# Outputs from a decayed state by quarters of the array, and short chunks with two heads stacked, in a fused retention and two-layer kernel

## The chip, the cores and the metric

The kernel runs on one core of a Trainium2 chip. The metric is the device time of one execution in microseconds (us). Before the change it is 884.49 us, the median of 3 runs (883.37 to 885.73).

## What is computed

Retention with a decay per head, its output laid out as 2304 tokens of 512, then two feed-forward layers. Everything is float32.

```python
def _attn_ref(q, k, v):                      # each (4, 8, 576, 64)
    scores = scale * np.matmul(q, k.transpose(0, 1, 3, 2))
    gamma = 1.0 - 2.0 ** (-5.0 - np.arange(H, dtype=np.float32))
    Dmat = np.where(rel >= 0, gamma[:, None, None] ** rel[None, :, :], 0.0)
    return np.matmul(scores * Dmat[None, :, :, :], v)

def _moe_ref(x, w_in, w_out, alpha):         # 512 -> 2048 -> 512
    h = x @ w_in
    g = np.maximum(h, 0.0) + alpha * np.minimum(h, 0.0)
    return g @ w_out

def _moe2_ref(x, w_gate, w_val, w_out):      # 512 -> 1536 -> 512
    gate = 1.0 / (1.0 + np.exp(-(x @ w_gate)))
    return (gate * (x @ w_val)) @ w_out
```

`reference` puts attention's heads beside each other, `x = attn_out.transpose(0, 2, 1, 3).reshape(B * S, H * D)`, and applies the two layers one after the other.

## The kernel before, in words

The 2304 tokens are cut into five blocks (256, then four of 512). Attention works in chunks of at most 128 positions of one sequence within one block, 20 in all; four of them have 64 positions (the end of a sequence of 576, or what a block leaves over). The first block has two chunks, the second five, the later ones four, five and four.

Within a sequence a chunk takes what lies before it from a state of 64x64 per head, kept in `m_sb`. Heads go in four pairs: one head of a pair on partitions 0 to 63, the other on 64 to 127. Before, `m_sb` holds for each pair a 128x128 block with the two heads' states on its diagonal and zeros elsewhere (cleared once, L1132). A chunk runs through these steps:

- `load_qk`, `load_kv` (L461 to L485): q and k with the head's dimensions on the partitions, k and v with the positions on the partitions. A short chunk fills 64 columns of each 128 in `qk`, and 64 partitions of `kv`.
- `att_q`, `att_v` (L488 to L500): POOL multiplies q by the decay and v by its inverse.
- `att_scores` (L502 to L518): TensorE forms k against q for each head, into two banks of PSUM (`s`), and VectorE multiplies both by the causal mask (L514).
- `att_values` (L520 to L563): the outputs from the state (L529, 128x128 operands, one per pair), the sums k against v that update it (L535, tile `m`), VectorE's additions to `m_sb` (L543, or copies for a sequence's first chunk, L545), ScalarE's scaling of `m_sb` by the decay over the chunk (L549), the outputs from the chunk itself (L553), and the split of the output (`split`, L198 to L204) into a high and a low part, one on ScalarE (L200) and one on VectorE (L201).

The layers' matmuls all come from one helper, `products` (L633): three products of high and low parts in the fp32r type. `h` is the first layer's inner value and turns in the two banks of `ps_h`; `y` is its output. A matmul of two float32 operands leaves two records in the trace.

What stands around the chunks differs. `att_run` (L594) takes the seven chunks of the first two blocks one after the other, the scores two chunks ahead, each with banks of its own: the pairs of banks rotate, one pair of `ps_a` and twice two of `ps_y`. Beside them it begins to prepare the first layer's weights: `weight_step` (L439) collects credit, and from the chunk with index `WITH` on (L60, L1160) each step adds 0.34 of a weight. A weight arrives as 512 KB in one of five raw slots (`r`), goes through ScalarE (L223, L224) and VectorE (L227, L229), is split into two parts (L246, L248), and frees its slot. The later three blocks' chunks run in the middle of the first layer (`att_stages`, L580): scores behind one `y`, the rest behind the next `h`.

TensorE's instructions run in the order of the code. The order of the others' queues is set by a scheduler in the compiler, which places an instruction where it expects its inputs; every queue runs strictly in order.

Of the kernel before, what the change touches and what calls it, by code (L numbers as in the profile page):

```python
# [10 lines left out]
F32 = mybir.dt.float32  # L11
# [3 lines left out]
AF = mybir.ActivationFunctionType  # L15
ALU = mybir.AluOpType
# [3 lines left out]
P = 128  # L20
B, H, S, D = 4, 8, 576, 64
NPAIR = H // 2
NT = B * S
DM = 512
KC = DM // P
NF1 = 2048 // P
# [17 lines left out]
PLAIN = 3  # L44
# [12 lines left out]

BEHIND = 2

WITH = 3  # L60


PACE_B, PACE_C = 0.34, 0.5
# [29 lines left out]
O_M = NPAIR * P  # L93
O_GK = O_M + P
O_GP = O_GK + H
N_CST = O_GP + len(LENGTHS) * NPAIR


def constants():
    gamma = (1.0 - 2.0 ** (-5.0 - np.arange(H, dtype=np.float32))).astype(np.float64)  # L100
    i = np.arange(P)
    head = 2 * np.arange(NPAIR)[None, :] + (i // D)[:, None]
    out = np.zeros((P, N_CST), np.float32)
    out[:, :O_M] = (gamma[head][:, :, None] ** i / np.sqrt(D)).reshape(P, -1)
    out[:, O_M:O_GK] = i[None, :] >= i[:, None]
    out[:, O_GK:O_GP] = gamma ** -i[:, None].astype(np.float64)
    out[:, O_GP:] = (gamma[head][:, None, :] ** np.array(LENGTHS)[None, :, None]).reshape(P, -1)
    return out


# [1 line left out]
def retention_two_ffn(ctx: ExitStack, tc: tile.TileContext, att, cst, alpha, w1, w2, out0, out1):  # L112
# [17 lines left out]
    xp = x_only.enter_context(tc.tile_pool(name="xp", bufs=2, side="right"))  # L130
    att_only = ctx.enter_context(ExitStack())
    ap = att_only.enter_context(tc.tile_pool(name="ap", bufs=1))
    c_sb = ap.tile([P, N_CST], F32, tag="c", name="c_sb")
    al_sb = const.tile([P, NF1], F32, tag="al", name="al_sb")
    na_sb = const.tile([P, NF1], F32, tag="na", name="na_sb")
    m_sb = ap.tile([P, NPAIR, P], F32, tag="m", name="m_sb")
# [313 lines left out]
    o = 0  # L450
# [10 lines left out]
    def load_qk(n):  # L461
        if n >= len(CHUNKS):
            return
        c = CHUNKS[n][3]
        half = 2 * c * H * D
        qk = slot([P, 2, NPAIR, P], F32, f"qk{n}")
        a = offset[n]
        src = att[a:a + half].rearrange("(p t a i) -> p t a i", p=P, t=2, a=NPAIR)
        if n == 0:
            nc.sync.dma_start(out=c_sb, in_=cst)  # L470
            nc.sync.dma_start(out=qk[:, :, 0:2, :c], in_=src[:, :, 0:2])
            nc.sync.dma_start(out=qk[:, :, 2:4, :c], in_=src[:, :, 2:4])
        else:
            nc.sync.dma_start(out=qk[:, :, :, :c], in_=src)
        raw_a[n] = [qk, None]

    def load_kv(n):
        if n >= len(CHUNKS):
            return
        c = CHUNKS[n][3]  # L480
        half = 2 * c * H * D
        kv = slot([P, 2, H * D], F32, f"kv{n}")
        a = offset[n] + half
        nc.sync.dma_start(out=kv[:c], in_=att[a:a + half].rearrange("(p t d) -> p t d", p=c, t=2))
        raw_a[n][1] = kv  # L485

    x_t = {}
# [6 lines left out]

    def att_v(n):

        c = CHUNKS[n][3]
        v = raw_a[n][1][:c, 1, :].rearrange("p (h d) -> p h d", h=H)
        gk = c_sb[:c, O_GK:O_GP]
        nc.gpsimd.tensor_tensor(out=v, in0=v, in1=gk.unsqueeze(2).to_broadcast([c, H, D]), op=ALU.mult)  # L500

    def att_scores(n, pool, tags):  # L502

        c = CHUNKS[n][3]
        qk = raw_a[n][0]
        ps = [pool.tile([P, NPAIR, P], F32, tag=tags[e], name=f"s{n}_{e}") for e in range(2)]
        for pr in range(NPAIR):
            for e in range(2):
                r = slice(e * D, (e + 1) * D)
                nc.tensor.matmul(ps[e][:c, pr, :c], qk[r, 1, pr, :c], qk[r, 0, pr, :c], start=True, stop=True)  # L510

        s_sb = qk[:, 1], small.tile([P, NPAIR, P], F32, tag="s", name=f"sc{n}")
        for e in (1, 0):
            nc.vector.tensor_tensor(  # L514
                out=s_sb[e][:c, :, :c], in0=ps[e][:c, :, :c],
                in1=mask[:c, :c].unsqueeze(1).to_broadcast([c, NPAIR, c]), op=ALU.mult,
            )
        return s_sb  # L518

    def att_values(n, s_sb, pool, tags):  # L520

        j, _, pos, c, col = CHUNKS[n]
        qk, kv = raw_a[n]
        last = pos + c == S
        o_ps = pool.tile([P, NPAIR, P], F32, tag=tags[0], name=f"o{n}")

        if pos:
            for pr in range(NPAIR):
                nc.tensor.matmul(o_ps[:, pr, :c], m_sb[:, pr, :], qk[:, 0, pr, :c], start=pr == 0, stop=False)  # L529
        if not last:  # L530
            m_ps = pool.tile([P, NPAIR, D], F32, tag=tags[1], name=f"m{n}")
            for pr in range(NPAIR):
                for e in range(2):
                    h = 2 * pr + e
                    nc.tensor.matmul(  # L535
                        m_ps[e * D:(e + 1) * D, pr, :], kv[:c, 0, h * D:(h + 1) * D],
                        kv[:c, 1, h * D:(h + 1) * D], start=True, stop=True,
                    )
            for e in range(2):
                r = slice(e * D, (e + 1) * D)  # L540
                dst = m_sb[r, :, e * D:(e + 1) * D]
                if pos:
                    nc.vector.tensor_tensor(out=dst, in0=dst, in1=m_ps[r], op=ALU.add)  # L543
                else:
                    nc.vector.tensor_copy(dst, m_ps[r])  # L545

            for pr in range(NPAIR):
                g = O_GP + LENGTHS.index(c) * NPAIR + pr
                nc.scalar.activation(m_sb[:, pr, :], m_sb[:, pr, :], AF.Copy, scale=c_sb[:, g:g + 1])  # L549
        for pr in range(NPAIR):  # L550
            for e in range(2):
                h = 2 * pr + e
                nc.tensor.matmul(  # L553
                    o_ps[e * D:(e + 1) * D, pr, :c], kv[:c, 1, h * D:(h + 1) * D], s_sb[e][:c, pr, :c],
                    start=pos == 0 and pr == 0, stop=pr == NPAIR - 1,
                )
        x = x_t[j]
        if j < PLAIN:
            split(x[:, 0, :, col:col + c], x[:, 1, :, col:col + c], o_ps[:, :, :c], True)
        else:  # L560
            urgent["act"].append(nc.scalar.activation(x[:, :, col:col + c], o_ps[:, :, :c], AF.Copy))
        free(qk)
        free(kv)  # L563

# [564 lines left out]
        split(g[:, 0], g[:, 1], ps[1])  # L1129
        return g  # L1130

    nc.gpsimd.memset(m_sb, 0.0)  # L1132
    for n in runs_of(0) + runs_of(1):
        load_chunk(n)
    nc.sync.dma_start(out=al_sb, in_=alpha)
# [269 lines left out]
```

## Time and profile before

| | |
|---|---|
| median of 3 runs | 884.49 us |
| profiled execution | 882.25 us, span 880.1 us |
| TensorE busy | 854.5 us (97%) |
| VectorE, ScalarE, POOL busy | 523.7, 445.1, 115.6 us |
| DMA | 245.00 MB, mean 278 GB/s |

The span runs from the first to the last instruction of the trace. A group of rows is read from the left: time of start, duration, engine, line, operation, what it writes and reads with shapes, how many. What stands in brackets is the time in which the engine was idle ahead of the row, and the instruction whose end released it.

### The profile page before, as it was taken

What the parts mean: (1) busy time and instruction counts of PE and PEld (TensorE: products, weight loads), DVE (VectorE), ACT (ScalarE), POOL (GpSimd) and SP (SyncE); (2) the same over time, 40 slices, a digit from 0 to 9 for tenths busy, and PEclk for the clock granted to TensorE, in tenths of its full rate; (3) what the DMA queues carried; (4) which work ended last, traced back from release to release, by engine and by line L of the source; (5) the groups of instructions that cost most, each with busy time, mean ns of one, the idle gap of its engine ahead of it and who ended that gap; (6) DMA issues with size and microseconds to landing.
All of it is one profiled execution on the core that took longest, in us unless ns stands there. A gap on an engine that the chain in (4) does not pass through costs nothing.

```text
span 880.1 us, 13000 instructions
## 1 busy us (share of the span) xinstructions
PE 854.5 (97%) x4770; PEld 717.7 (82%) x4770; DVE 523.7 (59%) x761; ACT 445.1 (51%) x785; POOL 115.6 (13%) x119
## 2 busy tenths in 40 slices
PE   5789999999999999999999999999999999999998
PEld 5678888888777888878888888887888888888897
DVE  3777774566676658979736565369833333596121
ACT  2698874455564567888525654345332222353111
POOL 6000002444411001115302131000000000000000
PEclk9899999999999999999999999999999999999999
DMA  9879989799996357777996999635697563359970
GB/s 310 284 280 375 383 287 418 294 346 292 352 335 211 132 196 264 253 289 265 380 386 225 384 419 394 272 108 204 238 396 274 191 192 120 139 210 355 394 265 25
DMA packets 89679, 245.00 MB, mean 278 GB/s; under 512 B 13072, under 2 KB 16144, under 8 KB 89616
## 3 DMA queue, kind: packets, MB, share of 16 engines
q1 hardware_dynamic: 89616, 244.17, 75.9%
q8 instruction: 38, 0.62, 0.3%
q14 instruction: 25, 0.20, 0.1%
HBM read 175.98 MB, written 68.16 MB: 277 GB/s over the span
## 4 chain that ended last, share of the span: by engine, by line
PE 81%; DMA 5%; DVE 5%; ACT 5%; issue 2%; SPq 1%; DVEq 0%; ACTq 0%
PE a L633 15%; PE yy L633 10%; PE h L633 9%; PE y L633 8%; PE oa L633 7%; PE z L633 4%; PE b L633 4%; PE e L633 4%; PE c L633 3%; DMA r<-w 3%; PE o L633 2%; PE oc L633 2%; PE ob L633 2%; PE oe L633 2%; PE a_h L633 2%
## 5 line engine op out<-in xcount | busy, mean ns | idle before, releaser
L633 PE MATMUL h<-x,w 128*128 128x512 f32 (+1 forms) x432 | 84.2, 347 | 4.1 <-DVE g L201 3.4
L633 PEld LDWEIGHTS h<-x,w 128*128 128x128 f32 x432 | 67.4, 189 | 15.0 <-DVE g L201 4.4
L302 POOL TENSOR_TENSOR r<-r,r 128x256 f32<-128x256 f32 x36 | 37.8, 1057 | 235.0 <-DVE r L229 225.4
L313 DVE TENSOR_TENSOR q<-r,q 128x512 fp32r<-128x512 f32 x72 | 52.8, 759 | 19.1 <-ACT q L312 18.9
L649 DVE SCALAR_TENSOR_TENSOR h<-h,na_sb,t 128x512 f32<-128x512 f32 (+1 forms) x48 | 32.0, 667 | 48.8 <-ACT h L648 48.8
L633 PE MATMUL y<-g,w 128*128 128x512 f32 x240 | 58.9, 394 | 0.0
L312 ACT ACTIVATE q<-r 128x512 fp32r<-128x512 f32 x72 | 45.6, 666 | 22.3 <-POOL r L302 11.8
L647 ACT ACTIVATE t<-h 128x512 f32<-128x512 f32 (+1 forms) x48 | 25.2, 524 | 61.3 <-PE h L633 61.2
L223 ACT ACTIVATE r<-r 128x512 f32<-128x512 f32 x68 | 45.4, 668 | 20.2 <-DMA r<-w 20.1
L633 PEld LDWEIGHTS y<-g,w 128*128 128x128 f32 x240 | 44.3, 188 | 10.2 <-issue 1.0
L959 DVE TENSOR_TENSOR c<-a,es 128x512 f32<-128x512 f32 x24 | 16.7, 698 | 55.9 <-PE a L633 55.9
L224 ACT ACTIVATE r<-r 128x512 int32<-128x512 uint32 x68 | 45.5, 669 | 0.0
L493 POOL TENSOR_TENSOR qk<-qk,c_sb 128x512 f32<-128x512 f32 (+1 forms) x21 | 24.7, 1178 | 153.3 <-DVE h L649 120.3
L229 DVE CUSTOM_DVE_ANT_0 r<-r,top 128x1024 uint16<-128x1024 uint16 x52 | 37.0, 721 | 2.7
L633 PEld LDWEIGHTS z<-x,zp 128*128 128x128 f32 x288 | 36.0, 191 | 0.9
L633 PE MATMUL z<-x,zp 128*128 128x256 f32 x288 | 36.3, 283 | 0.0
L201 DVE TENSOR_TENSOR g<-h,g 128x512 fp32r<-128x512 f32 (+1 forms) x48 | 28.8, 599 | 12.5 <-ACT g L200 12.0
L200 ACT ACTIVATE g<-h 128x512 fp32r<-128x512 f32 (+1 forms) x48 | 25.2, 524 | 20.8 <-DVE h L649 19.9
L633 PE MATMUL h<-x,v 128*128 128x512 f32 x144 | 35.4, 395 | 0.0
L633 PE MATMUL y<-g,v 128*128 128x512 f32 x144 | 35.1, 393 | 0.0
L302 POOL TENSOR_TENSOR r<-r 128x256 f32<-128x256 f32 x36 | 32.1, 896 | 11.6 <-DVE r L229 10.4
L227 DVE TENSOR_SCALAR top<-r 128x512 uint32<-128x512 uint32 x52 | 24.0, 470 | 13.4 <-ACT r L223 11.6
(457 smaller groups left out, 2199.4 us busy)
## 6 DMA issues: line engine op xcount, KB each, us to landing
tq<-td SPq DMA_DIRECT2D x84, 512.0 KB, 9.0
r<-w SPq DMA_DIRECT2D x68, 512.0 KB, 6.8
wo<-wod SPq DMA_DIRECT2D x42, 512.0 KB, 3.6
v<-w1d SPq DMA_DIRECT2D x40, 512.0 KB, 6.4
td<-q SPq DMA_DIRECT2D x36, 512.0 KB, 4.8
w1d<-w SPq DMA_DIRECT2D x32, 512.0 KB, 7.6
wod<-q SPq DMA_DIRECT2D x24, 512.0 KB, 9.5
zp<-td SPq DMA_DIRECT2D x48, 256.0 KB, 5.2
```

Source lines behind the costliest of these rows:

```text
L200: a = nc.scalar.activation(hi, src, AF.Copy)
L201: d = nc.vector.tensor_tensor(out=lo, in0=src, in1=hi.bitcast(F32), op=ALU.subtract)
L223: nc.scalar.activation(high.bitcast(F32), high.bitcast(F32), AF.Prelu, scale=2.0 ** -112, alpha=2.0 ** 32)
L224: nc.scalar.activation(low.bitcast(I32), low, AF.Copy, scale=2.0 ** -29)
L229: nc.vector.tensor_tensor(out=out.bitcast(I32), in0=low.bitcast(I32), in1=top.bitcast(I32), op=ALU.add)
L302: sub = lambda o, a, b: nc.gpsimd.tensor_tensor(out=o, in0=a, in1=b, op=ALU.subtract)
L312: nc.scalar.activation(part[0], src, AF.Copy)
L313: nc.vector.tensor_tensor(out=part[1], in0=src, in1=part[0].bitcast(F32), op=ALU.subtract)
L493: nc.gpsimd.tensor_tensor(out=q, in0=q, in1=decay[:, part, :c], op=ALU.mult)
L633: nc.tensor.matmul(ps, l, r, start=first and i == 0, stop=last and i == len(todo) - 1, skip_group_check=joins)
L647: nc.scalar.activation(t, ps, AF.Relu)
L649: nc.vector.scalar_tensor_tensor(ps, ps, na_sb[:, f:f + 1], t, ALU.mult, ALU.add)
```

## The change

- The state is kept without its zeros: `m_sb` is 128x(4x64), and its update is an addition and a scaling of the whole tile, both on VectorE. ScalarE's scaling and the clearing on POOL go.
- The outputs from the state are formed head by head with 64x64 operands instead of pair by pair. The output of an odd pair is changed over: its first head is written to partitions 64 to 127 and the second to 0 to 63. Even and odd pairs go to two banks, so that four heads in a row use the four quarters of the array. The rows of the first layer's input weights are put in the order that matches, on the host.
- The output of a chunk lies in two banks and is split in two halves. The sums `m` move to the banks of `ps_h`, and ahead of the outputs from the state.
- Short chunks have two heads stacked on the partitions in `kv` and in the scores: one bank and one masking instead of two, full partitions for v, and a `qk` tile without gaps. They have constants of their own (a stacked mask, a stacked decay: 68 more columns).
- `WITH` is 4, not 3.

```diff
-WITH = 3
+WITH = 4
@@ load_qk, load_kv
-        qk = slot([P, 2, NPAIR, P], F32, f"qk{n}")
+        qk = slot([P, 2, NPAIR, c], F32, f"qk{n}")
...
-            nc.sync.dma_start(out=qk[:, :, :, :c], in_=src)
+            nc.sync.dma_start(out=qk, in_=src)
...
-        kv = slot([P, 2, H * D], F32, f"kv{n}")
+        kv = slot([P, 2, H * c // P, D], F32, f"kv{n}")
@@ att_scores
+        if c < P:
+            ps = pool.tile([P, NPAIR, c], F32, tag=tags[0], name=f"s{n}")
+            for pr, e in HEADS:
+                nc.tensor.matmul(ps[part(e), pr, :], qk[part(e), 1, pr, :], qk[part(e), 0, pr, :], start=True, stop=True)
+            by = c_sb[:, O_M2:O_GK2].unsqueeze(1).to_broadcast([P, NPAIR, c])
+            nc.vector.tensor_tensor(out=qk[:, 1], in0=ps, in1=by, op=ALU.mult)
+            return qk[part(0), 1], qk[part(1), 1]
@@ att_values
-        o_ps = pool.tile([P, NPAIR, P], F32, tag=tags[0], name=f"o{n}")
+        o_ps = [pool.tile([P, 2, c], F32, tag=t, name=f"o{n}_{i}") for i, t in enumerate(tags)]
+        out = lambda pr, e: o_ps[pr % 2][part(e ^ pr % 2), pr // 2, :]
+        rows = lambda t, pr, e: kv[part(e), t, pr] if c < P else kv[:, t, 2 * pr + e]
+        if not last:
+            m_ps = ps_h.tile([P, NPAIR, D], F32, tag="h", name=f"m{n}")
+            for pr, e in HEADS:
+                nc.tensor.matmul(m_ps[part(e), pr, :], rows(0, pr, e), rows(1, pr, e), start=True, stop=True)
         if pos:
-            for pr in range(NPAIR):
-                nc.tensor.matmul(o_ps[:, pr, :c], m_sb[:, pr, :], qk[:, 0, pr, :c], start=pr == 0, stop=False)
+            for pr, e in HEADS:
+                nc.tensor.matmul(
+                    out(pr, e), m_sb[part(e), pr, :], qk[part(e), 0, pr, :], start=pr < 2, stop=False,
+                )
         if not last:
...
+            if pos:
+                nc.vector.tensor_tensor(out=m_sb, in0=m_sb, in1=m_ps, op=ALU.add)
+            nc.vector.tensor_tensor(out=m_sb, in0=m_sb if pos else m_ps, in1=by, op=ALU.mult)
...
-            split(x[:, 0, :, col:col + c], x[:, 1, :, col:col + c], o_ps[:, :, :c], True)
+                to = x[:, :, i::2, col:col + c]
+                split(to[:, 0], to[:, 1], ps, i == 1)
@@ host
+    w_in = np.stack([w_in[i, ::-1] if i % 2 else w_in[i] for i in range(NPAIR)])
```

Here `part(i)` is the i-th half of the partitions, and `HEADS` lists the pairs and the two heads of each.

VectorE's queue before, from the scores of the fourth chunk on (`sc` and `qk` are its masked scores; `one` and `r` belong to the first weight, `x` is a split output):

```order
L514 TENSOR_TENSOR sc_355<-s_1_346,c_sb 128x512
L514 TENSOR_TENSOR qk_212<-s_0_345,c_sb 128x512
L227 TENSOR_SCALAR one_0_435<-r_0_0_229 128x512
L543 TENSOR_TENSOR m_sb<-m_sb,m_365 64x4x64 x2
L229 ISA one_0_435<-r_0_0_229,one_0_435 128x1024
L201 TENSOR_TENSOR x_299<-o_360,x_299 128x4x128
```

The same place of the queue now:

```order
L531 TENSOR_TENSOR sc_355<-s_1_346,c_sb 128x512
L531 TENSOR_TENSOR qk_211<-s_0_345,c_sb 128x512
L561 TENSOR_TENSOR m_sb<-m_sb,m_362 128x256
L562 TENSOR_TENSOR m_sb<-m_sb,c_sb 128x256
L206 TENSOR_TENSOR x_296<-o_0_360,x_296 128x2x128
L206 TENSOR_TENSOR x_296<-o_1_361,x_296 128x2x128
L232 TENSOR_SCALAR one_0_475<-r_0_0_228 128x512
L524 TENSOR_TENSOR qk_215<-s_393,c_sb 128x256
L234 ISA one_0_475<-r_0_0_228,one_0_475 128x1024
L253 TENSOR_TENSOR w_0_0_492<-one_0_475,w_0_0_492 128x512
L561 TENSOR_TENSOR m_sb<-m_sb,m_407 128x256
L562 TENSOR_TENSOR m_sb<-m_sb,c_sb 128x256
```

The third state update (`m_365` before, `m_362` now) and its chunk's split have moved ahead of the first weight's first instruction; the fourth update (`m_407`) now stands behind that weight's last one.

TensorE's queue before, in the eighth chunk, the first of the third block (`h_12` is the matmul ahead of it):

```order
L633 MATMUL h_12_1809<-x_299,v_0_1753 128x512 x12
L529 MATMUL o_1833<-qk_1743,m_sb 128x128 x4
L535 MATMUL m_1838<-kv_1745 64x64 x8
L553 MATMUL o_1833<-qk_1743,kv_1745 64x128
L553 MATMUL o_1833<-sc_1800,kv_1745 64x128
```

The same place now:

```order
L647 MATMUL h_12_1817<-x_296,v_0_1761 128x512 x12
L550 MATMUL m_1843<-kv_1753 64x64 x8
L553 MATMUL o_0_1841<-qk_1751,m_sb 64x128 x2
L553 MATMUL o_1_1842<-qk_1751,m_sb 64x128 x2
L553 MATMUL o_0_1841<-qk_1751,m_sb 64x128 x2
L553 MATMUL o_1_1842<-qk_1751,m_sb 64x128 x2
L564 MATMUL o_0_1841<-qk_1751,kv_1753 64x128
L564 MATMUL o_0_1841<-sc_1808,kv_1753 64x128
```

The sums are first now, and four matmuls from the state have become eight of half the width, in turn into two tiles.

## Rows read from the trace of the kernel before

**Rows 1.** Busy time by stretch: busy us and instructions per engine, granted clock, DMA.
```profile
23.40:28.70 5.30, 0.00 (x1) 0.00 (x1) 3.29 (x8) 4.37 (x9) 0.92 (x1) 0.90 1.00 397
28.70:38.60 9.90, 9.90 (x128) 8.93 (x128) 7.32 (x15) 5.45 (x14) 0.00 (x0) 0.71 0.76 251
...
40.00:60.00 20.00, 17.44 (x122) 14.70 (x121) 16.07 (x32) 18.84 (x43) 0.00 (x0) 1.00 0.76 256
77.00:146.00 69.00, 68.26 (x416) 61.34 (x417) 49.19 (x91) 51.40 (x106) 1.29 (x1) 1.00 0.95 353
146.00:285.00 139.00, 137.03 (x1071) 111.13 (x1070) 86.03 (x142) 75.55 (x155) 48.34 (x49) 1.00 0.87 311
```

**Rows 2.** Timeline of the first hole, all engines.
```profile
24.33 0.65 ACT L223 ACTIVATE r<-r 128x512 f32<-128x512 f32 x1 [3.34 <-DMA r<-w]
25.01 0.43 DVE L227 TENSOR_SCALAR one<-r 128x512 uint32<-128x512 uint32 x1 [2.11 <-ACT r L223]
25.36 0.86 DVE L543 TENSOR_TENSOR m_sb<-m_sb,m 64x256 f32<-64x256 f32 x2
26.25 0.69 DVE L229 CUSTOM_DVE_ANT_0 one<-r,one 128x1024 uint16<-128x1024 uint16 x1
...
28.25 1.27 ACT L549 ACTIVATE m_sb<-m_sb,c_sb 128x128 f32<-128x128 f32 x4
28.70 2.07 PE L529 MATMUL o<-qk,m_sb 128*128 128x128 f32 x8 [5.32 <-ACT m_sb L549]
...
29.42 1.14 ACT L246 ACTIVATE w<-one 128x512 fp32r<-128x512 f32 x2
```

**Rows 3.** Timeline: the fifth chunk's read, the last split, the second block's h.
```profile
35.01 1.10 PE L529 MATMUL o<-qk,m_sb 128*128 128x64 f32 x8
...
45.02 0.42 DVE L201 TENSOR_TENSOR x<-o,x 128x256 fp32r<-128x256 f32 x1
...
45.50 0.73 PE L633 MATMUL h<-x,w 128*128 128x512 f32 x2 [0.71 <-DVE x L201]
```

**Rows 4.** Attention's tiles: duration in ns min/median/max, first and last start.
```profile
L529 PE MATMUL o<-qk,m_sb x128: 218/275/581, 16.5 to 279.9; 128*128 128x128 f32 x104, 128*128 128x64 f32 x24
L549 ACT ACTIVATE m_sb<-m_sb,c_sb x64: 384/391/407, 13.3 to 273.8; 128x128 f32<-128x128 f32 x64
L543 DVE TENSOR_TENSOR m_sb<-m_sb,m x24: 402/420/426, 18.3 to 271.8; 64x256 f32<-64x256 f32 x24
...
L200 ACT ACTIVATE x<-o x11: 377/580/602, 14.4 to 188.0; 128x512 fp32r<-128x512 f32 x9, 128x256 fp32r<-128x256 f32 x2
L201 DVE TENSOR_TENSOR x<-o,x x11: 417/691/693, 15.0 to 188.6; 128x512 fp32r<-128x512 f32 x9, 128x256 fp32r<-128x256 f32 x2
```

**Rows 5.** DMA packets, from 14 to 22 us and from 24 to 28 us.
```profile
DMA packets 2801, 2.65 MB, mean 332 GB/s; under 512 B 2286, under 2 KB 2286, under 8 KB 2800
...
DMA packets 455, 1.65 MB, mean 414 GB/s; under 512 B 51, under 2 KB 51, under 8 KB 455
```

**Rows 6.** Timeline: the weight with the least to spare and its first use.
```profile
129.63 0.69 DVE L248 TENSOR_TENSOR w<-r,w 128x512 fp32r<-128x512 f32 x1 [0.28 <-ACT w L246]
...
136.71 0.88 PE L633 MATMUL y0a<-g,w 128*128 128x256 f32 x6
```

**Rows 7.** Timeline of TensorE in the eighth chunk.
```profile
157.44 1.05 PE L529 MATMUL o<-qk,m_sb 128*128 128x128 f32 x8
...
158.42 0.69 PE L535 MATMUL m<-kv 128*64 128x64 f32 x16
...
158.94 0.28 PE L553 MATMUL o<-qk,kv 128*64 128x128 f32 x1
...
159.05 0.27 PE L553 MATMUL o<-qk,kv 128*64 128x128 f32 x1
```

**Rows 8.** Timeline: the split that frees h's bank, and the next h.
```profile
254.53 0.69 DVE L201 TENSOR_TENSOR g<-h,g 128x512 fp32r<-128x512 f32 x1 [0.66 <-ACT g L200]
...
255.25 3.02 PE L633 MATMUL h<-x,w 128*128 128x512 f32 x12
```

More of the change, by code (lines that the diff above doesn't have):

```diff
@@ L132, in retention_two_ffn @@
     ap = att_only.enter_context(tc.tile_pool(name="ap", bufs=1))
+    m_sb = ap.tile([P, NPAIR, D], F32, tag="m", name="m_sb")
     c_sb = ap.tile([P, N_CST], F32, tag="c", name="c_sb")
@@ L495, in att_v, with part @@
     def att_v(n):
[L497 to L500, printed above, removed]
+        v = raw_a[n][1][:, 1]
+        heads = v.shape[1]
+        gk = O_GK if heads == H else O_GK2
+        by = c_sb[:, gk:gk + heads].unsqueeze(2).to_broadcast([P, heads, D])
+        nc.gpsimd.tensor_tensor(out=v, in0=v, in1=by, op=ALU.mult)
+    def part(i):
+        return slice(i * D, (i + 1) * D)
+    HEADS = [(pr, e) for pr in range(NPAIR) for e in range(2)]
     def att_scores(n, pool, tags):
@@ L505, in att_scores @@
         qk = raw_a[n][0]
+        if c < P:
[5 more added lines that the diff above has]
+            return qk[part(0), 1], qk[part(1), 1]
         ps = [pool.tile([P, NPAIR, P], F32, tag=tags[e], name=f"s{n}_{e}") for e in range(2)]
-        for pr in range(NPAIR):
-            for e in range(2):
-                r = slice(e * D, (e + 1) * D)
-                nc.tensor.matmul(ps[e][:c, pr, :c], qk[r, 1, pr, :c], qk[r, 0, pr, :c], start=True, stop=True)
+        for pr, e in HEADS:
+            nc.tensor.matmul(ps[e][:, pr, :], qk[part(e), 1, pr, :], qk[part(e), 0, pr, :], start=True, stop=True)
         s_sb = qk[:, 1], small.tile([P, NPAIR, P], F32, tag="s", name=f"sc{n}")
@@ L527, in att_values @@
         if pos:
-            for pr in range(NPAIR):
-                nc.tensor.matmul(o_ps[:, pr, :c], m_sb[:, pr, :], qk[:, 0, pr, :c], start=pr == 0, stop=False)
+            for pr, e in HEADS:
+                nc.tensor.matmul(
+                    out(pr, e), m_sb[part(e), pr, :], qk[part(e), 0, pr, :], start=pr < 2, stop=False,
+                )
         if not last:
[L531 to L556, printed above, removed]
-        x = x_t[j]
-        if j < PLAIN:
-            split(x[:, 0, :, col:col + c], x[:, 1, :, col:col + c], o_ps[:, :, :c], True)
-        else:
-            urgent["act"].append(nc.scalar.activation(x[:, :, col:col + c], o_ps[:, :, :c], AF.Copy))
+            g = O_GP + LENGTHS.index(c) * NPAIR
@@ new lines, in att_values @@
+            by = c_sb[:, g:g + NPAIR].unsqueeze(2).to_broadcast([P, NPAIR, D])
+            if pos:
+                nc.vector.tensor_tensor(out=m_sb, in0=m_sb, in1=m_ps, op=ALU.add)
+            nc.vector.tensor_tensor(out=m_sb, in0=m_sb if pos else m_ps, in1=by, op=ALU.mult)
+        for pr, e in HEADS:
+            nc.tensor.matmul(
+                out(pr, e), rows(1, pr, e), s_sb[e][:, pr, :], start=pos == 0 and pr < 2, stop=pr >= 2,
+            )
+        x = x_t[j]
+        for i, ps in enumerate(o_ps):
+            if j < PLAIN:
+                to = x[:, :, i::2, col:col + c]
+                split(to[:, 0], to[:, 1], ps, i == 1)
+            else:
+                a = nc.scalar.activation(x[:, i::2, col:col + c], ps, AF.Copy)
```

30 lines of the change are left out of this document (19 added, 11 removed).

## The prediction

> **What bounds the kernel now.** I read the busy time by stretch first, then the timeline of the first 46 us, then the engine groups of the attention tiles, then one chunk in the middle. By the stretches [rows 1] TensorE is busy for 68.26 of 69 us (77 to 146 us) and for 137.03 of 139 (146 to 285). From about 77 us on the program is as long as what TensorE still has to do, so a saving counts in two ways only: TensorE reaches that point earlier, or it has less to do later. Before it there is one large hole: from 23.40 to 28.70 us TensorE does nothing, and in the 9.9 us behind it its granted clock is 0.71 on average, that is between its two levels of 1.2 and 2.4 GHz.
>
> The timeline shows what fills the hole [rows 2]. The first weight lands at 24.33 us and ScalarE starts on it, 3.34 us idle before. VectorE's next instruction (L227) belongs to that weight and waits for ScalarE until 25.01. Queued behind it stands the state update of the fourth chunk (L543, 25.36), then ScalarE scales the state (28.25, behind three weights' conversions), and only then TensorE reads it (28.70, 5.32 us idle). The attention of the first two blocks ends with the split of the last chunk's output on VectorE at 45.02, and TensorE takes the second block's first h at 45.50, after 0.71 us of waiting for it [rows 3].
>
> **The change, part by part.**
>
> *The state update.* Before, each chunk that hands on a state has two VectorE additions of 64x256 at 420 ns and four ScalarE scalings at 391 ns that start about 0.3 us apart, 1.27 to 1.28 us in all [rows 2, 4]. Now VectorE adds and scales 128x256 in two instructions. 128x256 has no row for this operation; on half the partitions the same width takes 420 ns, and the split of a 128x256 tile takes 420 ns as well [rows 3, 4], so I take 0.42 each: VectorE pays the same, ScalarE pays nothing. Sixteen chunks: 64 x 0.391 = 25 us off ScalarE. The splits of the output become two of half the width: ScalarE from 580 to 2 x 0.38, VectorE from 691 to 2 x 0.42 (the shortest rows of both are the half width, 377 and 417 [rows 4]), 0.15 to 0.18 us more per chunk on each. Beyond the first 60 us neither engine bounds, so both are worth nothing there.
>
> *The first hole.* The order of VectorE shows what matters: the first weight instruction now stands behind the third state update, not ahead of it, and the update needs no ScalarE. So chunks one to four run through, and the hole moves one chunk on, to the fifth chunk's read of the state. How late is that? The two short chunks ahead of the weights were loaded in small packets: 8 us with 2286 of them (14 to 22 us) moved 2.65 MB, where 4 us without moved 1.65 MB [rows 5]; at that rate 2.65 MB take 6.4 us. They are loaded in full rows now. Of the 1.6 us I take 1.0, since other packets are in it: first weight at 23.3 (bounds 22.7 and 24.33). From there, by order and by the durations of [rows 2]: ScalarE's two passes 0.65 each (24.6), VectorE's combine 0.69 (25.3); ScalarE's conversion waits for the second weight's two passes (25.9) and takes 0.57 (26.5); VectorE's subtraction 0.69 [rows 6], its addition and scaling 0.42 each, each begun as the one before ends: the state is ready at 28.0. Before, the same chunk's read of the state started at 35.01 [rows 3]: 7.0 us earlier.
>
> From there VectorE bounds up to the last split. By its order it has between the two points the splits of four chunks (4 x 0.42, and 4 of a quarter's width, about 0.27), three masks (2 x 0.69, as wide as the full split, and 0.42), two state updates (3 x 0.42 in all), two subtractions and two combines (4 x 0.69), two first weight steps (2 x 0.43), and one h (2 x 0.42): 10.3 us. With 0.5 for waits the second block's first h then starts at about 38.8, against 45.50: 6.7 us. A price is left on this lead. In the new order one weight fewer is prepared at that point, 2 x 0.65 + 0.57 = 1.9 us of ScalarE, and ScalarE is busy for 18.84 of 20 us from 40 to 60 [rows 1]; its lost scalings (1.27 in that stretch) pay for most. I keep **6.5 us**, bounds 2.5 and 8.5. Weights don't take it back: the one with the least to spare is ready at 129.63 + 0.69 = 130.32 and first used at 136.71 [rows 6] (found by counting along the order of both engines), 6.4 us later, and their preparation moves forward as well.
>
> *The outputs from the state.* In the middle a chunk has, from start to start [rows 7]: 0.98 us for the state's outputs (157.44 to 158.42), 0.52 for the state's sums (16 records, 0.0325 each), then pairs 0.11 apart for the values. The eight records of the first kind are 0.111 apart (1.05 less one of 0.275, by seven [rows 4, 7]), so they need 0.89, and 0.09 goes into the change of operand shape. Now there are 16 records of a quarter each. No row shows four quarters at once. Bounds: at the sums' pace (two column halves, 64 columns streamed) 0.52; at the values' pace, two at a time, 0.88; one after the other 16 x 0.111 = 1.78. I take 0.52, since the quarters are as independent as the halves and the records at 0.0325 show that the queue feeds that fast. But the shapes now change four times per chunk and not twice (h, sums, state, values, y), 0.1 each: 0.98 less the old change is 0.89, less 0.52 and less twice 0.1 more is 0.17, about **0.2 us** per chunk: for ten full chunks behind 146 us, and next to nothing for the short ones, **1.9 us**.
>
> The Trainium skill ("TensorEngine Tiling (Array Packing)", Key Properties) says that a change of tiling mode, not of tile, drains the engine; the trace agrees as far as the 0.09 goes. By that rule alone, with a full record of 0.275 drained at each of the two added changes, the ten chunks would lose 0.2 each instead of winning 0.2.
>
> *The bank for the sums.* m moves from the attention's banks to the two that h turns in. So the next h needs the bank of the h before it, not of the one before that. At its tightest, the split that frees it ends at 254.53 + 0.69 = 255.22 and the next h starts at 255.25 [rows 8], already with only 0.03 to spare; ScalarE's missing 1.28 us moves the split forward, TensorE's saving moves h forward by 0.2. I put **0.3 us** on it, bounds 0 and 7.
>
> *Nothing to gain or lose:* the memset of the state (POOL waits for its first data anyway), the shorter scalings of v on POOL, the weights' rows changed over on the host, 68 more columns of constants (35 KB).
>
> Sum: -6.5 - 1.9 + 0.3 = -8.1 us. The profiled execution took 882.25 us, 880.1 of it the span; the median of the runs is 884.49, 2.24 above it. So 874.2 for a run like the profiled one, and **876.4 us** as the median.
>
> **The rivals.**
>
> *Two quarters at a time.* For it: every pair of this trace that shares an engine runs so, none runs four. Against: the pairs are made of two halves only, nothing else was asked. The state's outputs then take 0.88 + 0.2 against 0.98, 0.1 more per chunk: -6.5 + 1.0 + 0.3, 879.3 us. The Trainium skill ("TensorE: Matmul & The Clock Gate", The mechanism) says that a weight load overlaps running matmuls only in another row group, which would hold the quarters of one row half apart; the sums' 0.0325 per record with loads in the same rows speaks against it here.
>
> *The lead is given back.* ScalarE is full from 40 to 60 us and has a weight more to prepare, VectorE has it too. For it: TensorE waits on h's splits there already. Against: ScalarE's scalings are gone and every weight has over 6 us to spare. With 3 us of the 6.5 left: -3 - 1.9 + 0.3, 879.9 us; with 1 left, 881.9.
>
> *The bank of h binds.* If h's split comes 0.7 us later against the next h in each of the ten chunks behind 146 us that hand on a state, and none has anything to spare, 7 us return: 883.1, no change. For it: the 0.03 above. Against: ScalarE loses work just ahead of that split.
>
> *The quarters run one after the other* (the slower side). Then the state's outputs take 1.78 + 0.2 against 0.98, 1.0 more in each of ten full chunks, and the start loses some 2.5 of its lead on the same instructions: -4 + 10 + 0.3, 890.8 us. It decides from the point where ten times (16 records + 0.2 - 0.98) eats 6.5 us: 0.089 us per record. Against it: halves that share rows or columns overlap everywhere in the trace.
>
> **How the numbers follow.** Forecast 0.56, two at a time 0.14, lead given back 0.13, bank of h 0.07, one after the other 0.05; 0.05 for better than all this (a lead of 8.5 and 0.4 per chunk: 872). The forecast's own range is 872 to 880. For 8 in 10 I take 870.5 to 882.5, which holds the first three, and leaves out the bank of h, the slower side and the ends. A measurement of this kernel can tell 0.3% from no change, 2.65 us: faster is below 881.8. The forecast, two at a time, better, and most of the lead given back make 0.83; the rest of that and the bank of h 0.10; slower 0.07.
>
> **What the profile will show.** Right: TensorE's hole sits ahead of the fifth chunk's read of the state at about 28 us; the second block's first h starts near 39; the 16 records of the state's outputs take about 0.5 us in the middle, the chunk about 0.2 less; TensorE is as full as before behind 77 us. Wrong: h waiting for splits behind each chunk (bank), new waits of h for w or g between 40 and 77 us (lead), records 0.055 or 0.11 apart (quarters). A hole that stays in front of the fourth chunk would overthrow the main term.

## The result and the profile after

The changed kernel takes 875.97 us, the median of 4 runs (874.78 to 876.75), beside 883.93 us for the kernel before on the same chip (4 runs, 883.14 to 885.73): a ratio of 0.9906, 95% interval 0.9886 to 0.9926. The forecast was 876.4 us. It is faster, by 8.0 us in the medians.

The two profiled executions lie closer together: 876.75 us after (span 875.0, the slowest of the four) against 882.25 (span 880.1), 5.5 us. What follows reads where these two differ, so it has 5.2 us to account for, not 8.0.

First the stretches of [rows 1] in the changed kernel; the columns are those of that group (PE, PEld, DVE, ACT, POOL).

```profile
23.40:28.70 5.30, 3.54 (x95) 3.04 (x92) 3.86 (x9) 3.46 (x9) 0.00 (x0) 1.00 0.98 388
28.70:38.60 9.90, 8.44 (x121) 7.17 (x117) 9.26 (x24) 6.98 (x20) 0.00 (x0) 1.00 0.68 223
40.00:60.00 20.00, 17.77 (x99) 15.19 (x98) 14.16 (x27) 16.39 (x34) 0.00 (x0) 1.00 0.91 318
77.00:146.00 69.00, 68.34 (x418) 60.89 (x418) 45.26 (x85) 47.53 (x99) 3.44 (x3) 1.00 0.98 366
146.00:285.00 139.00, 133.74 (x1145) 104.35 (x1142) 90.59 (x142) 64.77 (x127) 46.70 (x48) 1.00 0.85 309
```

The hole has no stretch of its own any more: TensorE works 3.54 of the 5.30 us in which it stood still, and its granted clock is 1.00 (2.4 GHz) where it was 0.71 behind the hole. VectorE is busy for 9.26 of 9.90 us: it is what most of the start now waits for, as forecast. But from 146 to 285 us TensorE is busy for 133.74 us, where it was 137.03. Part of that is work saved, part is new idle time.

The timeline of the start (start, duration, engine, line, what is written and read, in brackets the idle time and what ended it) answers to [rows 2, 3].

```profile
23.13 0.68 ACT L228 ACTIVATE r<-r 128x512 f32<-128x512 f32 x1 [0.56 <-DMA r<-w]
23.24 0.67 PE L553 MATMUL o<-qk,m_sb 64*64 64x128 f32 x16
...
26.77 0.41 DVE L561 TENSOR_TENSOR m_sb<-m_sb,m 128x256 f32<-128x256 f32 x1
27.21 0.42 DVE L562 TENSOR_TENSOR m_sb<-m_sb,c_sb 128x256 f32<-128x256 f32 x1
27.79 0.46 PE L553 MATMUL o<-qk,m_sb 64*64 64x64 f32 x16 [1.76 <-DVE m_sb L562]
28.22 0.68 DVE L531 TENSOR_TENSOR sc<-s,c_sb 128x512 f32<-128x512 f32 x1
28.82 0.68 DVE L531 TENSOR_TENSOR qk<-s,c_sb 128x512 f32<-128x512 f32 x1
...
36.20 0.43 ACT L205 ACTIVATE x<-o 128x128 fp32r<-128x128 f32 x2
36.51 0.49 DVE L206 TENSOR_TENSOR x<-o,x 128x128 fp32r<-128x128 f32 x2 [0.47 <-ACT x L205]
36.52 5.85 PE L647 MATMUL h<-x,w 128*128 128x512 f32 x24 [0.18 <-ACT x L205]
```

The first weight is there at 23.13 (24.33 before, forecast 23.3), the fourth chunk reads the state at 23.24 without a wait (28.70 before), the hole stands ahead of the fifth chunk and is 1.76 us long (5.32 before), its state is ready at 27.63 (forecast 28.0), and the second block's first h starts at 36.52.

An h is 12 products of TensorE. The row of [rows 3] at 45.50 is not this one's start: the row ahead of it holds 12 products of the first block and one more, which by the single records is this h's first, at 44.39.

```profile
42.87 1.92 PE L633 MATMUL h<-x,w 128*128 128x256 f32 x13
```

The second product waited for VectorE's part of the split. Like with like, the first product goes from 44.39 to 36.52, 7.87 us earlier, and the second from 45.50 to 36.86 (single record), 8.64 us earlier; the forecast's 38.8 belongs to the second. The last 2.3 us ahead of this h stand on ScalarE, not on VectorE: its part of the split (36.20) is queued behind a weight's conversion and two passes (from 34.54), and VectorE's part waits 0.47 us for it.

In the middle one chunk looks so on TensorE; it answers to [rows 7].

```profile
149.68 0.69 PE L550 MATMUL m<-kv 128*64 128x64 f32 x16
150.29 0.67 PE L553 MATMUL o<-qk,m_sb 64*64 64x128 f32 x16
150.89 0.32 PE L564 MATMUL o<-qk,kv 128*64 128x128 f32 x1
...
151.91 3.01 PE L647 MATMUL y<-g,w 128*128 128x512 f32 x12
```

The 16 records of the state's outputs start 0.027 us apart in the mean, (0.67 - 0.27) / 15 with 0.27 for one, a quarter of the 0.111 between two full records before. By the single records they start in fours: four within 0.02 us, the next four 0.16 later, then 0.11 and 0.11. That is what four quarters working at once leave; a_two, below, tests it. From start to start, medians over the full chunks (those of 128 positions) between 140 and 290 us that have the part:

| us per chunk | before | after |
|---|---|---|
| h ahead of the chunk | 2.857 | 2.948 |
| state's sums | 0.515 | 0.615 |
| outputs from the state | 0.982 | 0.597 |
| values | 0.976 | 1.024 |
| sum | 5.330 | 5.184 |

A chunk with all four parts takes 0.15 us less, as forecast (0.17). But the waits of TensorE from 139 to 280 us have grown. Rows are in us in total, times, longest; the kernel before has

```profile
PE o L529 <- DVE qk L514: 1.3, 3, 0.6
PE s L510 <- issue: 0.6, 1, 0.6
```

and the changed one

```profile
PE h L647 <- DVE g L206: 1.5, 1, 1.5
PE o L553 <- DVE qk L531: 1.5, 1, 1.5
PE s L528 <- DVE x L206: 1.0, 2, 0.6
PE s L522 <- POOL kv L508: 0.9, 1, 0.9
PE o L564 <- DVE qk L531: 0.4, 1, 0.4
```

that is 5.3 us instead of 1.9. Four products of TensorE that both kernels have show where the 5.2 us come from:

| start of | before | after | shift |
|---|---|---|---|
| second block's first h, second product | 45.50 | 36.86 | -8.64 |
| a y ahead of the middle | 150.68 | 142.83 | -7.85 |
| a y behind the middle | 281.09 | 274.76 | -6.33 |
| the last product's 12 records | 873.52 | 868.30 | -5.22 |

From 150 to 281 us seven of the ten full chunks have all four parts (-0.15 each), two have no sums (4.86 us before, 4.57 after, -0.29 each) and one reads no state (no change but for a wait): -1.6 in all. The two short chunks there, put at next to nothing by the forecast, give another 1.0: from a y to the next h 4.40 us before and 3.58 after in the one, 0.2 less in the other beside its wait. With 1.9 us of old waits gone and 5.3 of new ones this makes +0.8; measured is +1.5. The rows of waits leave out idle time that is scattered between the records of a group: the two waits of the scores (`s` for `x`), 0.4 and 0.6 us in the rows, cost 0.8 and 1.1 from the y to the next h. So such a sum is good to within some 0.7 us. Behind that, 1.1 go into waits of the second layer (0.6 us before and 1.2 after for the same DMA, `wo`, alone). So in the profiled execution the start gave more than forecast, and the middle took what it should have given.

Whose wait is the largest? VectorE's timeline ahead of the one for the masks (`qk`, 264.5 us):

```profile
257.33 0.42 DVE L232 TENSOR_SCALAR top<-r 128x512 uint32<-128x512 uint32 x1
260.57 0.69 DVE L343 TENSOR_TENSOR s<-b 128x512 f32<-128x512 f32 x1 [2.81 <-DMA b<-w1f]
...
263.10 0.68 DVE L531 TENSOR_TENSOR sc<-s,c_sb 128x512 f32<-128x512 f32 x1
263.70 0.68 DVE L531 TENSOR_TENSOR qk<-s,c_sb 128x512 f32<-128x512 f32 x1
```

Line 343 forms sums of a weight for later blocks and waits 2.81 us for its DMA; the masks are queued behind it. The kernel before has the same queue and waits 2.1 us in it, but TensorE waited only 0.6 us for the masks there:

```profile
265.65 0.69 DVE L338 TENSOR_TENSOR s<-b 128x512 f32<-128x512 f32 x1 [2.09 <-DMA b<-w1f]
```

The wait of h (1.5) has another cause, here on VectorE and POOL:

```profile
226.58 4.89 DVE L318 TENSOR_TENSOR q<-r,q 128x512 fp32r<-128x512 f32 x3 [1.45 <-ACT q L317]
...
227.74 3.19 POOL L500 TENSOR_TENSOR qk<-qk,c_sb 128x512 f32<-128x512 f32 x2 [0.20 <-DMA qk<-att]
...
231.74 0.74 DVE L663 SCALAR_TENSOR_TENSOR h<-h,na_sb,t 128x512 f32<-128x512 f32 x1
```

Three VectorE instructions of 0.68 us each (the median of L318) take 4.89 while POOL works, and h's first step on VectorE (L663) comes only at 231.74, 2.8 us behind ScalarE's second step, which ended at 228.95. The next h (233.88) has to wait for that split, since the sums have taken the other of h's two banks: the forecast's rival "the bank of h binds", once.

### The profile page after: what moved, and what is told of

The parts are those of the page before. It is cut to its first block, busy times and chain, and to the rows that moved or that the text cites. A ratio compares the mean times of both kernels' runs of the same rounds, so it can differ in the third digit from the quotient of the medians.

```text
span 875.0 us, 13201 instructions
## 1 busy us (share of the span) xinstructions
PE 848.6 (97%) x4898; PEld 707.6 (81%) x4898; DVE 526.0 (60%) x764; ACT 427.3 (49%) x741; POOL 114.6 (13%) x118
## 4 chain that ended last, share of the span: by engine, by line
PE 78%; DMA 7%; DVE 6%; ACT 4%; issue 2%; SPq 1%; POOL 1%; DVEq 0%; ACTq 0%
PE a L647 15%; PE yy L647 10%; PE h L647 9%; PE y L647 8%; PE oa L647 7%; PE z L647 4%; PE b L647 4%; PE e L647 4%; PE c L647 3%; DMA r<-w 3%; PE o L647 2%; PE oc L647 2%; PE ob L647 2%; PE oe L647 2%; PE a_h L647 2%
## 5 line engine op out<-in xcount | busy, mean ns | idle before, releaser
L318 DVE TENSOR_TENSOR q<-r,q 128x512 fp32r<-128x512 f32 x72 | 55.7, 797 | 18.8 <-ACT q L317 18.8
L663 DVE SCALAR_TENSOR_TENSOR h<-h,na_sb,t 128x512 f32<-128x512 f32 (+1 forms) x48 | 32.0, 667 | 46.6 <-ACT h L662 46.2
L234 DVE CUSTOM_DVE_ANT_0 r<-r,top 128x1024 uint16<-128x1024 uint16 x52 | 39.3, 767 | 2.4
```

Source lines behind the costliest of these rows:

```text
L234: nc.vector.tensor_tensor(out=out.bitcast(I32), in0=low.bitcast(I32), in1=top.bitcast(I32), op=ALU.add)
L318: nc.vector.tensor_tensor(out=part[1], in0=src, in1=part[0].bitcast(F32), op=ALU.subtract)
L663: nc.vector.scalar_tensor_tensor(ps, ps, na_sb[:, f:f + 1], t, ALU.mult, ALU.add)
```

## The experiments

Shifts are those of the last three products of that table against the kernel before, in the profiled executions (us; before 150.68, 281.09, 873.52). The runs were made on several chips; each ratio is to the kernel before on the same chip, and so compares better than the medians do. The changed kernel has -7.85, -6.33, -5.22.

| run | median (runs) | ratio to before, 95% | shift at 150 | at 281 | at the end |
|---|---|---|---|---|---|
| b_with4 | 882.95 (12) | 0.9985 (0.9972 to 0.9997) | -1.48 | +0.36 | +0.42 |
| b_dve | 888.12 (6) | 1.0038 (1.0025 to 1.0051) | +3.34 | +4.31 | +4.06 |
| b_dve_with4 | 880.64 (5) | 0.9959 (0.9947 to 0.9971) | -2.62 | -2.06 | -1.54 |
| a_with3 | 881.77 (9) | 0.9971 (0.9959 to 0.9983) | -1.88 | -1.81 | -1.13 |
| a_act | 877.08 (5) | 0.9923 (0.9908 to 0.9938) | -4.60 | -5.03 | -3.83 |
| a_pack | 877.91 (4) | 0.9921 (0.9907 to 0.9936) | -5.13 | -3.13 | -3.37 |
| a_two | 877.00 (4) | 0.9911 (0.9897 to 0.9926) | -8.05 | -5.21 | -5.01 |
| a_two_banks | 879.00 (4) | 0.9925 (0.9902 to 0.9948) | -5.38 | -3.67 | -3.25 |
| a_order | 875.27 (5) | 0.9906 (0.9891 to 0.9921) | -8.00 | -4.72 | -4.43 |
| a_sfirst | 877.58 (4) | 0.9914 (0.9898 to 0.9929) | -7.47 | -6.70 | -6.45 |
| a_yield | 874.68 (4) | 0.9894 (0.9881 to 0.9908) | -7.05 | -10.25 | -8.12 |
| a_best | 875.01 (4) | 0.9894 (0.9880 to 0.9908) | -6.52 | -7.60 | -6.84 |

The changed kernel up to 150 us is the same program in a_yield, and its shift there differs by 0.8; less than that says nothing. Medians of the a-runs that differ by under 0.25% aren't told apart by their intervals.

### What makes the lead at the start

**Parts of the change put into the kernel before.** b_with4 begins the weights one chunk later:

```diff
-WITH = 3
+WITH = 4
```

> The kernel before with WITH = 4 alone. Theory 1: the state's update still goes over ScalarE; the hole moves one chunk on, the second block's first h starts 2 to 5 us earlier than at 45.5; total 879.5 to 882.5 us. Theory 2 (WITH alone): 7 to 9 us earlier, total 875 to 877.5 us. Theory 3: no change, 883 to 885 us.

b_dve scales the state on VectorE in one instruction of 128x512; b_dve_with4 does both.

```diff
-            for pr in range(NPAIR):
-                g = O_GP + LENGTHS.index(c) * NPAIR + pr
-                nc.scalar.activation(m_sb[:, pr, :], m_sb[:, pr, :], AF.Copy, scale=c_sb[:, g:g + 1])
+            g = O_GP + LENGTHS.index(c) * NPAIR
+            by = c_sb[:, g:g + NPAIR].unsqueeze(2).to_broadcast([P, NPAIR, P])
+            nc.vector.tensor_tensor(out=m_sb, in0=m_sb, in1=by, op=ALU.mult)
```

> The kernel before with the scaling of the state in one VectorE instruction of 128x512 instead of four on ScalarE, WITH = 3. Theory 1: the read of the state behind the first weight needs one queue less, 2 to 4 us earlier; ScalarE has 25 us less; total 880 to 882.5 us. Theories 2 and 3: no change, 883 to 885 us.

> The kernel before with both: scaling on VectorE and WITH = 4. Theory 1: nearly the whole lead, the second block's first h at 37 to 39.5 us, total 876 to 879 us, since only the packets (1 us) and the attention's shorter matmuls are missing. Theory 2: the same as WITH = 4 alone, within 1 us. Theory 3: 883 to 885 us.

The update on VectorE by itself makes the kernel slower. TensorE's waits up to 60 us in b_dve, then those in b_with4:

```profile
PE o L529 <- DVE m_sb L549: 10.8, 2, 8.9
```

```profile
PE h L633 <- DVE g L201: 3.5, 2, 2.4
PE o L529 <- ACT m_sb L549: 1.6, 2, 0.9
```

In b_dve the scaling stands on VectorE behind the first weight's steps and waits with them, 8.9 us at a time. So the theory that the update's move off ScalarE makes the lead fell as stated. In b_with4 the wait for the state is down to 1.6 us, and the second block's first h starts 5.2 us earlier (39.22, before 44.39); but by 62 us only 2.2 are left, while h waits for its split (2.4 us at a time) and the granted clock is 0.91 from 40 to 60 us, where it was 1.00: the forecast's rival "the lead is given back", in a kernel whose ScalarE still has the scalings to do. Both together keep what they win: -3.2 at the second block's first h (41.19), -2.62 at 150 us. That they would make nearly the whole lead was expected and is wrong: 4.7 us are missing at that h, and TensorE still waits 4.7 us for the state up to 60 us (four times, at most 2.4). The packets, below, are worth 2.7 there; what gives the rest (the narrower state, the stacked short chunks, the halved split) no run takes apart.

**Parts taken out of the changed kernel.** a_with3 goes back to `WITH = 3`; a_act has the scaling on ScalarE again, in four instructions of 128x64:

```diff
-            nc.vector.tensor_tensor(out=m_sb, in0=m_sb if pos else m_ps, in1=by, op=ALU.mult)
+            if not pos:
+                nc.vector.tensor_copy(m_sb, m_ps)
+            for pr in range(NPAIR):
+                nc.scalar.activation(m_sb[:, pr, :], m_sb[:, pr, :], AF.Copy, scale=c_sb[:, g + pr:g + pr + 1])
```

and a_pack loads the short chunks' q and k in small packets again:

```diff
-        qk = slot([P, 2, NPAIR, c], F32, f"qk{n}")
+        qk = slot([P, 2, NPAIR, P], F32, f"qk{n}")[:, :, :, :c]
```

> The changed kernel with WITH = 3 again, everything else kept. Theory 1 (the state's update without ScalarE makes the start faster, WITH only says which chunk meets the first weight): the second block's first h starts 3 to 5 us earlier than before instead of 7.9 to 8.7; total 878.5 to 881 us. Theory 2 (WITH alone makes the lead): it starts within 1.5 us of before, total 882.5 to 886 us. Theory 3 (the first weight's earlier arrival and the packets make the lead): as fast as the changed kernel, within 1 us of 876.

> The changed kernel, but the state is scaled by ScalarE again (four instructions of 128x64 per chunk, ahead of them VectorE's addition or copy); WITH=4, the quarters and the full packets stay. Theory (the lead needs the update off ScalarE's queue): the read of the state waits behind weights' conversions again, TensorE waits 3 to 6 us for m_sb from ScalarE, the lead at the second block's first h falls from 7.9 us to 2 to 5, and the time is 879 to 882. Rival (four chunks ahead of the weights and the full packets make the lead by themselves): lead 7 to 8, no such wait over 1 us, 876 to 877.5.

> The changed kernel with q and k of short chunks in tiles of 128 columns per pair again, so that they arrive in packets of 256 bytes. Theory P (the packets make 1 us of the lead): the first weight lands at 24.1 to 24.4 us instead of 23.1, the second block's first h about 1 us later, total 876.5 to 877.5 us. Theory O (the lead that is left beyond WITH comes from the packets altogether): 4 to 5 us later, 880 to 881 us.

The fourth chunk's read of the state in a_with3, timeline of VectorE and TensorE:

```profile
28.15 0.42 DVE L562 TENSOR_TENSOR m_sb<-m_sb,c_sb 128x256 f32<-128x256 f32 x1
28.72 1.13 PE L553 MATMUL o<-qk,m_sb 64*64 64x128 f32 x16 [6.64 <-DVE m_sb L562]
```

and the first weight, the fourth chunk's read and the fifth chunk's scaling in a_act:

```profile
21.89 1.06 ACT L564 ACTIVATE m_sb<-m_sb,c_sb 128x64 f32<-128x64 f32 x4 [2.14 <-DVE m_sb L560]
23.05 0.67 PE L553 MATMUL o<-qk,m_sb 64*64 64x128 f32 x16
23.39 0.69 ACT L228 ACTIVATE r<-r 128x512 f32<-128x512 f32 x1
...
27.42 1.06 ACT L564 ACTIVATE m_sb<-m_sb,c_sb 128x64 f32<-128x64 f32 x4 [1.15 <-DVE m_sb L560]
```

With `WITH = 3` the hole is where it was, 28.72 against 28.70, and 6.64 us long, although ScalarE has nothing to do with the state: the update stands behind the first weight on VectorE. With ScalarE scaling but `WITH = 4` the fourth chunk's read is not late at all (23.05), and the hole still moves on. So the later begin of the weights moves the hole, worth 6.0 us at 150 us; the scaling off ScalarE is worth 3.25 there, and the packets 2.7. These add to more than the lead of 7.85: each is worth that much only with the others in place. In the ratios a_with3 is slower than the changed kernel, and their intervals don't touch; a_act and a_pack, 1.5 and 1.3 us slower by their ratios, are not resolved.

The packets: DMA from 14 to 22 us in the changed kernel and in a_pack, answering to [rows 5].

```profile
DMA packets 1322, 3.27 MB, mean 409 GB/s; under 512 B 273, under 2 KB 273, under 8 KB 1321
```

```profile
DMA packets 2932, 2.71 MB, mean 339 GB/s; under 512 B 2280, under 2 KB 2280, under 8 KB 2931
```

The same 8 us move 3.27 MB instead of 2.71. In a_pack the first weight lands at 24.15 and the fifth chunk's state is ready at 28.68, 1.0 us later in both, just what the forecast put on the packets. But TensorE then waits 3.4 us there, not 1.76, its granted clock is 0.91 from 20 to 40 us where it was 1.00, and the second block's h is 2.7 us later (39.23). a_act, 2.3 us later at that h (38.86), has 0.98 and 0.85 in the same two stretches of ten.

### The quarters

a_two doesn't change odd pairs over: two quarters at a time, the rest as it is. a_two_banks moreover has one output bank, one split and the sums in the attention's bank, as before.

```diff
-        out = lambda pr, e: o_ps[pr % 2][part(e ^ pr % 2), pr // 2, :]
+        out = lambda pr, e: o_ps[pr % 2][part(e), pr // 2, :]
```

a_order sends each quarter its two products one behind the other:

```diff
-            for pr, e in HEADS:
+            for pr, e in sorted(HEADS, key=lambda x: (x[0] % 2, x[1])):
```

> The changed kernel with the odd pairs not changed over: heads use two quarters of the array in turn, the banks and everything else are kept. Theory Q (four quarters run at once in the changed kernel because they are four): a chunk's state outputs take 0.9 to 1.0 us instead of 0.60; ten full chunks in the middle, 3 to 4 us; total 879 to 880.5 us. Theory N (half the width alone makes it shorter): 0.60 as before, 876 us.

> As the run with two quarters, and the outputs in one bank again, split in one piece, the sums in the attention's other bank and not in h's. Theory B (the new waits in the middle come from the banks: scores that wait for the splits of both banks, h that waits for the sums' bank): the waits of 0.4 to 1.5 us between 140 and 275 us go, 2 to 3 us less than with two quarters alone, total 876.5 to 878.5 us. Theory L (they come from the lead: TensorE is early against the queues of POOL and VectorE): the same waits stay, total within 0.7 us of two quarters alone.

> The changed kernel, but the eight products of the state's outputs are sent so that each quarter of the array gets its two in a row instead of the quarters in turn. If a quarter works on its own and the queue runs ahead of a busy one: still 0.60 us per chunk from start to start and 876. If a second product for a busy quarter holds up those behind it: 0.8 to 1.0 us per chunk, 2 to 4 us over ten chunks as far as nothing else waits (with two quarters at a time 4 us of such time cost only 1 of the total): 876.5 to 879.

A chunk's outputs from the state in a_two, and in a_order:

```profile
150.09 1.09 PE L553 MATMUL o<-qk,m_sb 64*64 64x128 f32 x16
```

```profile
150.15 0.69 PE L553 MATMUL o<-qk,m_sb 64*64 64x128 f32 x16
```

Two quarters at a time take 0.055 us per record, (1.09 - 0.27) / 15, and 1.02 us from start to start, more than the 0.98 of the old form: without the change-over a full chunk would lose 0.28 us. Four take half of that in either order. In a_order, too, they start in fours, 0.11 apart, although the queue's first four records are for one quarter; that fits quarters which take their records past each other (the records don't name the quarter, so this is inferred). The Trainium skill ("TensorE: Matmul & The Clock Gate", The mechanism) says that a weight load overlaps running matmuls only where the row group differs, and in the same section that a load into the background weight buffer is pulled ahead as well. With the first alone the trace doesn't agree, the second would allow what it shows: in the changed kernel the loads for the second four start 0.05 us behind the first four matmuls, which are at work in both halves of the rows for the next 0.11 us. The 0.42 us per chunk between four and two are real, and a_two's shift loses 2.8 us between 150 and 281 us where the changed kernel's loses 1.5. Yet its ratio is only 0.0005 above the changed kernel's, 0.4 us, which the intervals don't resolve: its waits from 139 to 280 us are only 2.2 us instead of 5.3:

```profile
PE o L553 <- DVE qk L531: 1.8, 1, 1.8
PE o L564 <- DVE qk L531: 0.4, 1, 0.4
```

A slower TensorE that arrives later at what isn't ready would do this; no run shows that it is the reason. a_two_banks gave no clear answer: its waits in the middle sum up to 2.2 us as well, 0.7 of them still the scores' for the split, but its order of the start differs, too, and 2.5 us of its lead are gone before any of these chunks.

### Where the gain of the middle goes

a_sfirst puts the four lines that form the sums behind the outputs from the state. a_yield begins the sums of the weights one step later, so that the waiting instruction of VectorE stands behind the next masks; a_best does both.

```diff
     def prepare_sums(t):
-        b, s = raw_w.pop((1, t))
+        yield; b, s = raw_w.pop((1, t))
```

> The changed kernel with the outputs from the state ahead of the sums, which saves one change of operand shape per chunk (h, state, sums, values, y instead of h, sums, state, values, y with the sums and the values in the same shape). Theory C (a change of shape costs 0.1 us): 0.1 us less in each of the nine full chunks behind 140 us that have both, total 875 to 876 us. Theory D (the order matters through the queues: the state's update waits for nothing else either way): no change beyond 0.5 us.

> The changed kernel, but the sums of the second layer's weights are begun one step later, so that VectorE's subtraction that waits for a weight's DMA (2.8 us at 257.7) stands behind the next masks and not ahead of them. Theory (the gain per chunk in the middle is lost in waits that others' work on VectorE sets): TensorE's wait of 1.5 us for the masks at 264.5 is gone, nothing takes its place, the shift against the kernel before between 150 and 281 us becomes zero or negative instead of +1.5, and the time falls by 1 to 2 us to 874 to 875. Rival (each wait removed is replaced by the next one): same total wait in the middle, 875.5 to 877.

> The changed kernel with both the state's outputs ahead of the state's sums (0.15 us less per chunk from start to start) and the sums of the second layer's weights begun one step later. Theory: the 3.3 us of waits for masks that the outputs-first order had are gone (they came from the same DMA wait on VectorE), so 10 chunks give 1.5 us and the waits 1.5 more: 872 to 874. Rival (the state's read, now ahead of the sums, or other splits become the wait): 876 to 878, with as much waiting in the middle as outputs-first alone.

a_sfirst needs 5.04 us per chunk and not 5.18 (the sums 0.515 and the values 0.976 again: one dear change of shape fewer), and still its median isn't lower. Its waits from 146 to 300 us, then those of a_yield and of a_best from 139 to 280 (in a_sfirst and a_best without one more row of 0.2):

```profile
PE o L549 <- DVE qk L531: 3.3, 3, 2.4
PE h L647 <- DVE g L206: 1.4, 1, 1.4
PE s L528 <- DVE x L206: 1.1, 2, 0.6
```

```profile
PE s L528 <- DVE x L206: 1.0, 2, 0.5
```

```profile
PE h L647 <- DVE g L206: 1.5, 1, 1.5
PE s L528 <- DVE x L206: 1.1, 2, 0.6
PE s L522 <- POOL kv L508: 0.7, 1, 0.7
PE o L549 <- DVE qk L531: 0.4, 1, 0.4
```

With that instruction behind the masks, VectorE doesn't wait for `b` at all between 225 and 300 us. a_yield has 1.0 us of waits in the middle where the changed kernel has 5.3, and its shift goes from -7.05 to -10.25 between 150 and 281 us, -3.2 instead of +1.5. That is near what the sum asks for, -3.5: -1.6 and -1.0 for the chunks, -1.9 for the old waits, +1.0 for the new. So the gain per chunk is there, and this wait was one that ate it. Not all of a_yield's difference is its own: the waits for h and for `kv` are gone in it as well, which the edit doesn't touch directly, and they are there again in a_best (where the wait for masks has fallen from 3.3 to 0.4, as expected). Behind 281 us a_yield gives back 2.1. Its ratio, 0.9894 like a_best's, is the lowest of all, 1.1 us below the changed kernel's, but the intervals overlap: that it is faster isn't shown.

## Why the prediction was right

*The hole moves on to the fifth chunk*: right in place and time (state ready at 27.63, forecast 28.0; first weight 23.13, forecast 23.3). The reason given was wrong in part: "the update needs no ScalarE" doesn't move the hole (a_with3 has that, and the hole stays); beginning the weights a chunk later does (a_act).

*VectorE bounds up to the last split, 10.3 us and 0.5 of waits*: right in kind for most of the way, too long. From 27.63 to the h's second product at 36.86 it took 9.2, forecast 10.8. The 22 instructions are those counted, but durations were added up, and two that follow each other overlap: the masks above last 0.68 and start 0.60 apart. Over some 20 overlaps that makes about 1.6. The wait came once, 0.47 ahead of the last split, and there ScalarE's queue was the bound. The forecast also read 45.50 as the start of this h; it is its second product.

*Weights don't take the lead back*: right; none was waited for. The price kept on the lead, 0.2, was too low: 0.8 went between the second block's first h and 150 us (8.64 to 7.85). So this term, -6.5 within 2.5 and 8.5, came out at -7.85.

*The outputs from the state, -1.9*: the size per chunk was right (0.15 against 0.17), four quarters at once as chosen, two dear changes of shape more: h ahead of the chunk 0.09 and the sums 0.10 longer, the values 0.05. The ten full chunks gave 1.6 in sum, and the short ones, put at next to nothing, 1.0. The term failed all the same: it took it that TensorE is "as full as before behind 77 us". There the profiled execution lost 1.5 us between 150 and 281 where it should have won 1.9.

*The bank of the sums, 0.3 within 0 and 7*: the wait came once, 1.5 us, in place of [rows 8]'s 0.03 to spare, not in each chunk; and it came from VectorE slowed by POOL.

*The sum*, -8.1, met the medians' -8.0. In the pair of profiled executions the errors (1.35 us more at the start, 3.1 less in the middle: +1.5 for -1.9 + 0.3) and 1.1 us behind 281 leave -5.2; that the median agrees better than the parts is partly luck. How the parts stand in executions that left no trace stays open.

The rivals: two quarters at a time would have cost 0.28 us per chunk and not 0.1 (a_two: 5.61 against 5.33); one after the other was far off.

## What to carry over

Where a saving per step goes on a full engine, look for the waits that stand just behind it: TensorE won 1.6 us in ten chunks and met a queue on VectorE that waited 2.8 us for a DMA of no urgency. Put such a waiting instruction behind those that the full engine waits for. Where a hole is set by what stands ahead in a strict queue, changing when that work begins moves the hole, and making the late work cheaper or giving it another engine does not (a_with3); once it has moved, the cheaper work is worth something on top (a_act: 3.25 us).

## What was not expected of the hardware

VectorE and POOL slow each other: L318 lasts 0.683 us in the median and up to 1.779 in the changed kernel, and three of them 4.89 beside two of POOL's that took 3.19. The kernel before has this as well (its L313: median 0.684, up to 1.777), so the change didn't bring it; in the changed kernel h met it. The Trainium skill ("SBUF — State Buffer", SBUF: two separate sides) says that VectorE instructions with two inputs in SBUF and POOL's hold a pair of ports against each other, one instruction at a time; the trace agrees: L318 reads two such tensors, and the three end at 228.08, 229.78 and 231.48, each 0.55 us behind the end of a POOL instruction that ran beside it (227.53, 229.23, 230.93). The same distance, to within 0.01 us, stands behind all 159 instructions of this line that last over 0.8 us in the 14 traces kept here.

A record of a quarter takes its quarter as long as a full one takes the array (0.11 us), and four of them side by side do so in either order of the queue (0.027 and 0.028 us per record). A change between operand shapes costs 0.05 to 0.10 us here, but not each does: a_sfirst's sums take 0.515 behind outputs of another shape. Two VectorE instructions in a row overlap by about 0.08 us (the masks above), unless the second reads what the first wrote (L561 and L562, 0.44 apart at 0.41).
